# Five 128-row chunks instead of six 96-row chunks for k and v of the later batches, with kv of two batches moved by one iteration

## The chip, the cores and the metric

The kernel runs on one core of one Trainium2 chip. The metric is the device time in microseconds (us); lower is better. Each time quoted is a median of several executions. Engines are named as in the profile: PE is TensorE (PEld its weight loads), DVE is VectorE, ACT is ScalarE, POOL is GpSimd, SP is SyncE. "L144" is line 144 of the kernel file; the change adds lines, so the same line of code has another number after it.

## The reference

```python
# q, k, v: (8 batches, 8 heads, 576 tokens, 64), float32
kv  = np.einsum('bhsd,bhse->bhde', k, v)          # 64x64 per head, summed over 576 tokens
out = np.einsum('bhsd,bhde->bhse', q, kv)
rms = np.sqrt(np.mean(out * out, axis=-1, keepdims=True) + 1e-06)
x   = (out / rms * g_norm)                        # then put into (4608, 512)
y   = ((x @ w_a) * (x @ w_b)) @ w_out             # 512 -> 1536 -> 512
```

The change touches only the first line: the product of k and v of each head, and how k and v reach it.

## The kernel before: the parts that matter

The feed-forward part (FFN) works in nine strips of 512 tokens. The attention of batch s+1 is woven into strip s, so that its small matmuls and its work on the other engines hide under the FFN matmuls. Batches 0 and 1 are called early, the others late. k and v are loaded by POOL, which casts them from float32 to bf16 on the way, with the 576 tokens of a head as 96 partitions times 6 tokens:

```python
EC, EP = 6, 96
def load_heads(b, t, src, hs):
    nc.gpsimd.dma_start(out=t[:, hs, :, :],
        in_=src[b, hs].rearrange("h (t c) d -> t h c d", c=EC))

def load_late(b):                       # all of a late batch
    if b > EARLY:                       # wait until qT of the batch before has landed
        nc.gpsimd.tensor_copy(gate, qT[(b - 1) % 2][0:1, 0, 0:1])
    d = qs_d[b].rearrange("t (h d) -> t h d", h=H)
    for hs in (slice(0, NP), slice(NP, H)):
        nc.gpsimd.dma_start(out=d[:, hs, :], in_=q[b, hs].rearrange("h t d -> t h d"))
    load_heads(b, kt[b % NB], k, slice(0, H))      # NB = 3 buffers
    load_heads(b, vt[b % NB], v, slice(0, H))
# q goes to a bf16 copy in HBM (qs) and comes back by a DMA transpose into qT
```

kv of one pair of heads is a sum over the chunks. The two heads of a pair write different halves of the output's partitions:

```python
def kv(self, p, o):
    for c in range(EC):
        for j in range(2):
            nc.tensor.matmul(o[j * D : (j + 1) * D, :],
                lhsT=kt[self.b % NB][:, 2 * p + j, c, :],
                rhs=vt[self.b % NB][:, 2 * p + j, c, :],
                start=(c == 0), stop=(c == EC - 1))
```

With four pairs, a late batch needs 48 such matmuls, here called its kv block. The woven schedule of a strip has 16 iterations: the first 12 are FFN units of 8 matmuls each, the last 4 are output groups of 12:

```python
def slot(A, s, n):                      # called after the FFN work of iteration n
    k0, kn, xs = (4, 1, (6, 9, 11, 13)) if s < 3 else (2, 1, (4, 7, 10, 12))
    if n == k0: ...                     # the kv block, then its copy by ACT
    for p in range(NP):
        if n == xs[p]:                  # x(p): out of pair p into PSUM banks 4, 5; squares on ACT
            A.x(p, X[0]); A.psq(p, X[0])
        if n == xs[p] + 1:              # sum of squares on PE, 1/rms on ACT,
            A.pss(p, SS); A.pst(p, X[0])    # product on DVE, which frees banks 4, 5
```

Of the kernel before, what the change touches and what calls it, by code (L numbers as in the profile page):

```python
# [9 lines left out]
BF16 = mybir.dt.bfloat16  # L10
# [5 lines left out]
def kernel(  # L16
# [11 lines left out]
    nc = tc.nc  # L28

    B, H, S, D = q.shape  # L30
# [5 lines left out]
    NP = H // 2  # L36
# [5 lines left out]
    EC, EP = 6, 96  # L42
    EARLY = 2
# [5 lines left out]
    def sb(shape, dt, name):  # L49
        return pool.tile(shape, dt, name=name, tag=name)  # L50
# [5 lines left out]
    wb_v = moe_w_b.rearrange("(kc p) f -> p kc f", p=128)  # L56
    wo_v = moe_w_out.rearrange("(fc p) e -> p fc e", p=128)

    NB = 3
    kt = [sb([EP, H, EC, D], BF16, f"kt{i}") for i in range(NB)]  # L60
    vt = [sb([EP, H, EC, D], BF16, f"vt{i}") for i in range(NB)]
    qt = [sb([EP, H, EC, D], BF16, f"qt{i}") for i in range(EARLY)]

    qT = [sb([128, NP, S], BF16, f"qT{i}") for i in range(2)]
# [37 lines left out]
    def load_heads(b, t, src, hs):  # L102
        nc.gpsimd.dma_start(  # L103
            out=t[:, hs, :, :], in_=src[b, hs].rearrange("h (t c) d -> t h c d", c=EC)
        )

    def load_pair(b, p):
        hs = slice(2 * p, 2 * p + 2)
        load_heads(b, qt[b], q, hs)
        load_heads(b, kt[b % NB], k, hs)  # L110
        load_heads(b, vt[b % NB], v, hs)

    def load_ab(c0, c1):
        nc.gpsimd.dma_start(out=wa_t[:, :, c0:c1], in_=wa_v[:, :, c0:c1])
# [5 lines left out]
    def load_late(b):  # L120
        if b > EARLY:

            nc.gpsimd.tensor_copy(gate, qT[(b - 1) % 2][0:1, 0, 0:1])  # L123
        d = qs_d[b].rearrange("t (h d) -> t h d", h=H)
        for hs in (slice(0, NP), slice(NP, H)):
            nc.gpsimd.dma_start(out=d[:, hs, :], in_=q[b, hs].rearrange("h t d -> t h d"))  # L126
        load_heads(b, kt[b % NB], k, slice(0, H))
        load_heads(b, vt[b % NB], v, slice(0, H))

    def transpose_q(b):  # L130
        nc.sync.dma_start_transpose(qT[b % 2], qs_d[b])
# [2 lines left out]
    class Attn:  # L134
# [4 lines left out]

        def kv(self, p, o):  # L140

            for c in range(EC):
                for j in range(2):
                    nc.tensor.matmul(  # L144
                        o[j * D : (j + 1) * D, :],
                        lhsT=kt[self.b % NB][:, 2 * p + j, c, :],
                        rhs=vt[self.b % NB][:, 2 * p + j, c, :],
                        start=(c == 0),
                        stop=(c == EC - 1),
                    )  # L150

        def kv_out(self, ps, src):
# [77 lines left out]
    class Unit:  # L230
        n = 0
# [82 lines left out]
    def dummy(n, i, cols=STRIP):  # L314
        for _ in range(n):
            nc.tensor.matmul(
                P[:, i, 0:cols], lhsT=zeros[:, 0:128], rhs=zeros[:, 0:cols], start=True, stop=True
            )
# [15 lines left out]
    nc.vector.memset(ones, 0.0)  # L334
    for t in kvb:
        nc.vector.memset(t, 0.0)
    nc.vector.memset(ones[0:D, 0:D], 1.0 / D)
    nc.vector.memset(ones[D : 2 * D, D : 2 * D], 1.0 / D)
    for p in range(1, NP):
        load_pair(0, p)  # L340
# [8 lines left out]
    for p in range(NP):  # L349
        load_pair(1, p)  # L350
    load_late(2)

    X, SS = (4, 0), 6


    A = Attn(0)
# [9 lines left out]
    t = P[:, 2, :].bitcast(BF16)[:, 0:S].rearrange("q (c t) -> q c t", c=EC)  # L366
# [4 lines left out]
    for c in range(EC):  # L371
        nc.tensor.matmul(
            P[:, SS, 0 : 2 * D],
            lhsT=kc0[:, c, :],
            rhs=vc[:, c, :],
            start=(c == 0),
            stop=(c == EC - 1),
# [10 lines left out]
    for p in range(1, NP):  # L388
        i = X[p % 2]
        A.kv1(p, 3 - p % 2)  # L390
        A.kv1_out(p, 3 - p % 2, nc.vector.tensor_copy)
        A.pss(p - 1, SS)
        if p < NP - 1:
            if p == 1:
                dummy(1, 2 + p % 2)
            A.qtr(p + 1, 3 - p % 2)
            A.qtr_out(p + 1, 3 - p % 2)
            A.pst(p - 1, X[(p - 1) % 2])
            A.px(p, i)
            A.psq(p, i)  # L400
            dummy(1 if p == 1 else 2, 2 + p % 2)
# [30 lines left out]
    A = Attn(1)  # L432
# [30 lines left out]
    def slot(A, s, n):  # L463

        kb = P[:, 7, 0 : NP * D].rearrange("q (p e) -> q p e", e=D)
        k0, kn, xs = (4, 1, (6, 9, 11, 13)) if s < 3 else (2, 1, (4, 7, 10, 12))
        if k0 <= n < k0 + kn:
            for p in range((n - k0) * NP // kn, (n - k0 + 1) * NP // kn):
                A.kv(p, kb[:, p, :])
            if n == k0 + kn - 1:  # L470
                A.kv_out(slice(0, NP), kb)
        for p in range(NP):
            if n == xs[p]:
                A.x(p, X[0])
                A.psq(p, X[0])
            if n == xs[p] + 1:
                A.pss(p, SS)
                A.pst(p, X[0])

    for s in range(1, N_STRIP - 1):  # L480
        b = s + 1
        A = Attn(b) if b < B else None
        for n in range(FC + 4):
            if n >= FC:
                i = O if n % 2 == 0 else n_ab[0] % 3
                n_ab[0] += n % 2
                ffn_o(s, n - FC, i)
            elif s > 1 or n > 1:
                ffn_ab(s, n)
            if A:  # L490
                slot(A, s, n)
            if n == 8 and b + 1 < B:
                if s > 1:
                    transpose_q(b + 1)
                    if b + 2 < B:
                        load_late(b + 2)
                else:
                    load_late(3)
        if s == 1:
            transpose_q(3)  # L500
            load_late(4)
# [43 lines left out]
```

## Time and profile before

| | before |
|---|---|
| median of the first 3 executions | 323.02 us (322.78 to 323.4) |
| profiled span | 321.1 us |
| PE busy | 98% |
| kv block of a late batch, 48 matmuls | 0.88 us |
| wait of PE for v of batch 2 | 0.40 us |

The page of the kernel before. In the first part the columns are busy us, share of the span and number of instructions. The rows of the second part give the span in 40 slices of 8 us, in tenths busy (PEclk: tenths of the full clock that were granted).

```profile
span 321.1 us, 4773 instructions
...
PE 313.3 (98%) x1896; PEld 151.2 (47%) x1931; DVE 123.9 (39%) x215; ACT 125.3 (39%) x216; POOL 60.3 (19%) x82
...
PEclk9999999999999999999999999999999999999999
DMA  8999999796369999595597150003000200020002
```

PE is full from the second slice on, at full clock. The DMA engines are at 90% or more almost without a break until about 61 us. So a us counts if it is taken from PE's own stream, or from one of the few waits of PE that are left. The wait of PE that matters here, with its sum, count and longest in us:

```profile
PE P L144 <- DMA vt<-in_v_dram: 0.4, 1, 0.4
```

The chain of waits before, in order of time (start, length in us, and what held the chain), around batches 2 and 3. "PE P L144 x48" stands for 48 instructions of line 144 on PE that write P, the tile in PSUM. L144 is kv, L221 is x, L195 the sum of squares, L241 the FFN:

```profile
45.77 14.00 DMA vt<-in_v_dram
59.82 0.95 PE P L144 x48
...
64.33 0.24 PE P L221 x2
...
70.00 0.24 PE P L221 x2
...
73.94 0.36 PE P L221 x2
...
94.03 0.88 PE P L144 x48
...
104.14 0.24 PE P L221 x2
```

The DMA of v of batch 2 took from 45.77 us to its landing at 59.77 us, and the kv block of batch 2 (59.82 us) came after the wait for it. The block of batch 3 (94.03 us) followed on other PE work, and took 0.88 us. The first x of batch 2 took 0.24 us (64.33 us) and so did the second (70.00 us; for batch 3 it is the piece at 104.14 us); the third took 0.36 us (73.94 us).

The DMA view before, for 40 to 43 us (mostly packets of q, k and v of batch 1, 768 B written each), for 45 to 50 us (mostly packets of q of batch 2, 128 B), and for 58 to 60 us, where q1 (mostly the transpose of q) meets the end of v (on q0). Each line gives packets, MB, and the summed time of the packets as a share of 16 engines' time; it passes 100% where packets overlap on an engine:

```profile
q0 software_dynamic: 847, 0.60, 131.7%
```
```profile
q0 software_dynamic: 4598, 0.74, 201.4%
```
```profile
q1 hardware_dynamic: 1132, 0.29, 102.8%
q0 software_dynamic: 118, 0.08, 26.2%
```

### The profile page before, as it was taken

To read this page: it belongs to the slowest core of one execution; us is meant where nothing else is said; L and a number is where in the kernel's file an instruction comes from. 1 tells how busy PE (TensorE), PEld (TensorE's weight loads), DVE (VectorE), ACT (ScalarE), POOL (GpSimd) and SP (SyncE) were. 2 spreads that over 40 slices of the span, in tenths; PEclk is the share of its full clock that TensorE was granted. 3 is DMA by queue.
4 is the path that set the end of the run, shared out by engine and by line. 5 is a ranking of instruction groups with operands and counts; after the bars stand their busy time and mean duration, and the time that the engine had idled before them with its cause. 6 is when DMAs were issued, how large, how long until landed. Compare 5 with 4: busy or idle time off the path is not lost.

```text
span 321.1 us, 4773 instructions
## 1 busy us (share of the span) xinstructions
PE 313.3 (98%) x1896; PEld 151.2 (47%) x1931; DVE 123.9 (39%) x215; ACT 125.3 (39%) x216; POOL 60.3 (19%) x82
## 2 busy tenths in 40 slices
PE   8899999999999999999999999999999999999995
PEld 3444454444444444444444445444444444444443
DVE  3543344344234423452244424532354243313421
ACT  3633165354334433542355325433454233123310
POOL 8944870230041150410050000000000000000000
PEclk9999999999999999999999999999999999999999
DMA  8999999796369999595597150003000200020002
GB/s 179 196 196 199 201 179 230 140 136 117 96 92 162 119 162 216 63 160 113 140 109 115 65 133 8 0 35 99 2 0 0 100 33 0 25 90 20 0 35 98
DMA packets 69902, 32.61 MB, mean 102 GB/s; under 512 B 43639, under 2 KB 65399, under 8 KB 69879
## 3 DMA queue, kind: packets, MB, share of 16 engines
q0 software_dynamic: 49712, 18.44, 48.7%
q1 hardware_dynamic: 19810, 13.44, 16.3%
q10 hardware_dynamic: 356, 0.43, 0.4%
q8 instruction: 15, 0.25, 0.3%
q14 instruction: 9, 0.07, 0.1%
HBM read 37.75 MB, written 12.98 MB: 158 GB/s over the span
## 4 chain that ended last, share of the span: by engine, by line
PE 80%; DMA 13%; POOL 4%; issue 1%; ACT 0%; POOLq 0%
PE P L241 49%; PE P L291 26%; DMA wb_t<-in_moe_w_b_dram 6%; DMA vt<-in_v_dram 4%; PE P L221 2%; PE P L195 2%; DMA qt<-in_q_dram 2%; PE P L144 2%; DMA wo_t<-in_moe_w_out_dram 2%; POOL qs L126 1%; POOL kt L103 1%; POOL vt L103 1%; POOL wo_t L118 0%; POOL wa_t L344 0%; POOL wb_t L344 0%
## 5 line engine op out<-in xcount | busy, mean ns | idle before, releaser
L259 DVE TENSOR_TENSOR ab<-P,asb 128x512 bf16<-128x512 f32 x108 | 74.5, 692 | 124.9 <-PE P L241 123.9
L241 PE MATMUL P<-xt,wa_t 128*128 128x512 bf16 x422 | 111.2, 379 | 0.9 <-issue 0.2
L241 PE MATMUL P<-xt,wb_t 128*128 128x512 bf16 x419 | 110.0, 379 | 0.4
L291 PE MATMUL P<-wo_t,ab 128*128 128x512 bf16 (+1 forms) x433 | 97.3, 373 | 0.6
L255 ACT CAST asb<-P 128x512 bf16<-128x512 f32 x108 | 63.0, 585 | 81.9 <-PE P L241 80.5
L241 PEld LDWEIGHTS <-wb_t 128*128 128x128 bf16 x432 | 42.3, 98 | 51.2 <-DMA wb_t<-in_moe_w_b_dram 0.4
L291 PEld LDWEIGHTS <-ab 128*128 128x128 bf16 x444 | 43.1, 98 | 45.6
L241 PEld LDWEIGHTS <-wa_t 128*128 128x128 bf16 x432 | 41.7, 98 | 44.4 <-issue 0.5
L209 DVE SCALAR_TENSOR_TENSOR xt<-P,g_col,rs 128x288 bf16<-128x288 f32 x64 | 30.1, 513 | 24.2 <-ACT rs L199 24.2
L199 ACT ACTIVATE rs<-P,eps_t 128x576 f32<-128x576 f32 (+1 forms) x33 | 23.9, 726 | 21.2 <-PE P L195 17.2
L304 ACT COPY osb<-P 128x512 f32<-128x512 f32 x17 | 9.9, 585 | 48.6 <-PE P L291 46.8
L191 ACT ACTIVATE sq<-P 128x576 bf16<-128x576 f32 x31 | 20.2, 650 | 20.0 <-PE P L221 18.0
L306 DVE COPY osb<-P 128x512 f32<-128x512 f32 x18 | 12.4, 692 | 32.4 <-PE P L291 30.1
L126 POOL DMA_DIRECT2D qs<-in_q_dram x12 | 19.6, 1633 | 1.8 <-issue 1.7
L123 POOL COPY gate<-qT 1x1 bf16<-1x1 bf16 x5 | 0.9, 176 | 91.9 <-DMA qT<-qs 91.9
L195 PE MATMUL P<-sq,ones 128*128 128x288 bf16 x64 | 13.2, 286 | 0.5 <-ACT sq L191 0.4
L221 PE MATMUL P<-qT,kvb 128*128 128x288 bf16 x56 | 11.7, 286 | 0.0
L155 ACT CAST kvb<-P 64x256 bf16<-64x256 f32 (+1 forms) x20 | 6.0, 301 | 12.5 <-PE P L144 12.4
L195 PEld LDWEIGHTS <-ones 128*128 128x128 bf16 x64 | 6.2, 98 | 7.4 <-issue 0.4
L103 POOL DMA_DIRECT2D vt<-in_v_dram x13 | 9.1, 697 | 0.7 <-DMA qt<-in_q_dram 0.5
L103 POOL DMA_DIRECT2D kt<-in_k_dram x13 | 9.2, 705 | 0.1
L144 PEld LDWEIGHTS <-kt 96*64 96x64 bf16 x372 | 7.2, 112 | 3.9 <-issue 3.8
(46 smaller groups left out, 65.6 us busy)
## 6 DMA issues: line engine op xcount, KB each, us to landing
out_dram<-osb SPq DMA_DIRECT2D x23, 256.0 KB, 2.0
qs<-in_q_dram POOLq DMA_DIRECT2D x12, 288.0 KB, 6.7
kt<-in_k_dram POOLq DMA_DIRECT2D x6, 576.0 KB, 8.4
vt<-in_v_dram POOLq DMA_DIRECT2D x6, 576.0 KB, 10.8
out_dram<-osb SPq DMA_DIRECT2D x13, 128.0 KB, 2.3
wo_t<-in_moe_w_out_dram POOLq DMA_DIRECT2D x12, 128.0 KB, 6.0
wa_t<-in_moe_w_a_dram POOLq DMA_DIRECT2D x5, 256.0 KB, 9.3
wb_t<-in_moe_w_b_dram POOLq DMA_DIRECT2D x5, 256.0 KB, 9.9
```

The source lines that it names most:

```text
L103: nc.gpsimd.dma_start(out=t[:, hs, :, :], in_=src[b, hs].rearrange("h (t c) d -> t h c d", c=EC))
L126: nc.gpsimd.dma_start(out=d[:, hs, :], in_=q[b, hs].rearrange("h t d -> t h d"))
L144: nc.tensor.matmul(o[j * D : (j + 1) * D, :], lhsT=kt[self.b % NB][:, 2 * p + j, c, :], rhs=vt[self.b % NB][:, 2 * p + j, c, :], start=(c ...
L191: nc.scalar.activation(sq[p % 3], P[:, i0 : i0 + 2, 0:HF], AF.Square)
L195: nc.tensor.matmul(P[:, i0 + h, 0:HF], lhsT=ones, rhs=sq[p % 3][:, h, :], start=True, stop=True)
L199: nc.scalar.activation(rs[p % 3][:, h0:h1, :], P[:, i0 + h0 : i0 + h1, 0:HF], AF.Abs_reciprocal_sqrt, bias=eps_t,)
L209: nc.vector.scalar_tensor_tensor(out=xt[p][:, t0 : t0 + HF], in0=P[:, x0 + h, 0:HF], scalar=g_col, in1=rs[p % 3][:, h, :], op0=ALU.mult, o ...
L221: nc.tensor.matmul(P[:, i0 + h, 0:HF], lhsT=kvb[self.b % 2][:, p, :], rhs=self.qT[:, p, h * HF : (h + 1) * HF], start=True, stop=True,)
L241: nc.tensor.matmul(self.a if w is wa_t else self.b, lhsT=w[:, kc, self.fc * 128 : (self.fc + 1) * 128], rhs=xt[kc][:, t0 : t0 + STRIP], st ...
L255: nc.scalar.copy(self.t, self.a)
L259: nc.vector.tensor_mul(abt[self.s % 2][self.fc], self.b, self.t)
L291: nc.tensor.matmul(P[:, i, e0:e1], lhsT=abt[s % 2][fc][:, g * 128 : (g + 1) * 128], rhs=wo_t[:, fc, e0:e1], start=(fc == 0), stop=(fc == F ...
```

## The change

Its intent: a matmul is meant to cost by its columns, so the 576 tokens should go through in as few chunks as the 128 partitions allow. Four chunks of 128 tokens and a remainder of 64, padded by zeros to 128 rows, make 5 chunks instead of 6, so 40 matmuls per kv block instead of 48. As the loads get more packets, kv of batches 2 and 3 comes one iteration later, and with it their first x, x(0). One copy in the start moves from DVE to ACT.

```diff
-    NB = 3
-    kt = [sb([EP, H, EC, D], BF16, f"kt{i}") for i in range(NB)]     # vt alike
+    kt = [sb([EP, H, EC, D], BF16, f"kt{i}") for i in range(EARLY)]  # vt alike
+    LC = S // 128
+    ktl = [sb([128, H, LC + 1, D], BF16, f"ktl{i}") for i in range(2)]  # vtl alike
 ... in load_late
-        load_heads(b, kt[b % NB], k, slice(0, H))
-        load_heads(b, vt[b % NB], v, slice(0, H))
+        n = 128 * LC
+        for t, src in ((ktl[b % 2], k), (vtl[b % 2], v)):
+            nc.gpsimd.dma_start(out=t[:, :, 0:LC, :],
+                in_=src[b, :, 0:n].rearrange("h (t c) d -> t h c d", c=LC))
+            nc.gpsimd.dma_start(out=t[0 : S - n, :, LC, :],
+                in_=src[b, :, n:].rearrange("h t d -> t h d"))
 ... in kv
-            for c in range(EC):
+            if self.b < EARLY:
+                kk, vv, rows = kt[self.b], vt[self.b], [EP] * EC
+            else:
+                kk, vv, rows = ktl[self.b % 2], vtl[self.b % 2], [128] * (LC + 1)
+            for c, n in enumerate(rows):
 ... in the start
+    for t in ktl + vtl:
+        nc.vector.memset(t[S - 128 * LC :, :, LC, :], 0.0)
-        A.kv1_out(p, 3 - p % 2, nc.vector.tensor_copy)
+        A.kv1_out(p, 3 - p % 2, nc.scalar.copy if p == NP - 1 else nc.vector.tensor_copy)
 ... in slot
-        k0, kn, xs = (4, 1, (6, 9, 11, 13)) if s < 3 else (2, 1, (4, 7, 10, 12))
+        k0, kn, xs = (5, 1, (7, 9, 11, 13)) if s < 3 else (2, 1, (4, 7, 10, 12))
```

(Cuts are marked by lines that begin with "..."; lines are joined where that saves space.)

More of the change, by code (lines that the diff above doesn't have):

```diff
@@ L57 @@
     wo_v = moe_w_out.rearrange("(fc p) e -> p fc e", p=128)
-    NB = 3
-    kt = [sb([EP, H, EC, D], BF16, f"kt{i}") for i in range(NB)]
-    vt = [sb([EP, H, EC, D], BF16, f"vt{i}") for i in range(NB)]
+    kt = [sb([EP, H, EC, D], BF16, f"kt{i}") for i in range(EARLY)]
+    vt = [sb([EP, H, EC, D], BF16, f"vt{i}") for i in range(EARLY)]
+    LC = S // 128
+    ktl = [sb([128, H, LC + 1, D], BF16, f"ktl{i}") for i in range(2)]
+    vtl = [sb([128, H, LC + 1, D], BF16, f"vtl{i}") for i in range(2)]
     qt = [sb([EP, H, EC, D], BF16, f"qt{i}") for i in range(EARLY)]
@@ L109, in load_pair @@
         load_heads(b, qt[b], q, hs)
-        load_heads(b, kt[b % NB], k, hs)
-        load_heads(b, vt[b % NB], v, hs)
+        load_heads(b, kt[b], k, hs)
+        load_heads(b, vt[b], v, hs)
     def load_ab(c0, c1):
@@ L126, in load_late @@
             nc.gpsimd.dma_start(out=d[:, hs, :], in_=q[b, hs].rearrange("h t d -> t h d"))
-        load_heads(b, kt[b % NB], k, slice(0, H))
-        load_heads(b, vt[b % NB], v, slice(0, H))
+        n = 128 * LC
+        for t, src in ((ktl[b % 2], k), (vtl[b % 2], v)):
+            nc.gpsimd.dma_start(
+                out=t[:, :, 0:LC, :],
+                in_=src[b, :, 0:n].rearrange("h (t c) d -> t h c d", c=LC),
+            )
+            nc.gpsimd.dma_start(
+                out=t[0 : S - n, :, LC, :], in_=src[b, :, n:].rearrange("h t d -> t h d")
+            )
     def transpose_q(b):
@@ L145, in kv @@
                         o[j * D : (j + 1) * D, :],
-                        lhsT=kt[self.b % NB][:, 2 * p + j, c, :],
-                        rhs=vt[self.b % NB][:, 2 * p + j, c, :],
+                        lhsT=kk[0:n, 2 * p + j, c, :],
+                        rhs=vv[0:n, 2 * p + j, c, :],
                         start=(c == 0),
-                        stop=(c == EC - 1),
+                        stop=(c == len(rows) - 1),
                     )
```

## The prediction

> **What bounds the kernel.** TensorE. The page gives PE 98% busy at a granted clock of 0.998; DVE and ACT 39%. PE's waits are small: 0.4 us for the DMA of v, 0.4 for wb at 16.45 us, some more in the start. The DMA engines are full only until about 61 us. So only time in PE's stream counts, or the wait for v.
>
> **Removed.** In the chain of waits a kv block of a late batch (48 matmuls of 96x64) takes 0.88 us (0.95 in batch 2), 18.3 ns per matmul; the displayed 196 ns overlap. 40 at the same spacing is 0.73 us. The Trainium skill, "TensorE: Matmul & The Clock Gate", section "LDWEIGHTS (loading the stationary operand)", says that a weight load costs by its columns, not its rows; so 128 rows should cost what 96 do (no run here shows it yet). Saving 0.15 us x 6 = 0.9 us, all on the critical path.
>
> **Moved: kv of batch 2.** Before, PE waits 0.40 us at 59.42 for v of batch 2, which lands at 59.8. Now kv comes 8 FFN matmuls (1.73 us) later, at about 61.1. x(0) moves along. If v has landed by then, the 0.40 us goes.
>
> **Added: DMA packets.** k and v of a batch were 768 packets each, of 768 B written (1,536 read). Now they are 1,024 of 512 B plus 512 of 128 B. In the DMA view of 40 to 43 us the 768 B packets go at about 260 per us (0.20 MB written per us); at 45 to 50 us the 128 B packets of q go at about 870 per us. Estimate: 2.9 us per tensor becomes 2.6 + 0.6, so 0.6 us more for the two if alone. But output stores run from 51 us and the transpose of q moves packets from 58 us, so the last 128 B packets alternate with it. I estimate 0.6 to 2 us: v lands at 60.4 to 61.8, against a need at 61.1. Hence a wait of 0 to 0.7 us, 0.3 expected, in place of the 0.40. The Trainium skill, "DMA: Bandwidth & Descriptors", section "Specifications", gives 512 B as the least for line rate: the main part is just there, the remainder below. POOL issues about 3 us instead of 1.55 us per late batch; it has slack. Later batches are loaded some 30 us ahead: no effect.
>
> **Nothing from the rest.** Four memsets on DVE (about 0.3 to 0.6 us each) fit in its 3 us wait for q at the start. The last kv copy of batch 0: 204 ns for 64 columns on ACT against 210 on DVE, and DVE is free 0.05 us after the matmuls anyway. Even a gain would end in PE's wait for wb at 16.45 us: DMA bounds the start.
>
> **Sum.** 323.0 - 0.9 - 0.40 + 0.3 = 322.0 us. Range 321.2 to 322.9. Chances: faster by over 2% 0.01, within 2% 0.98, slower by over 2% 0.01.
>
> **What would show it.** Right: kv blocks of 40 matmuls in about 0.73 us; PE's wait before kv of batch 2 between 0 and 0.7 us; v's DMAs longer to landing; chain until 16.5 us as before. Wrong: blocks still 0.88 us (the spacing grows with rows); over 1 us of wait at kv of batch 2, or at its fifth chunk, which waits for the remainder's own DMA; PE waiting for k or v of a later batch.
>
> **What would make it wrong.** Small packets sharing the engines worse than estimated, so that v of batch 2 lands at 63 us or later; the transpose of q (landed 61.8 before) delayed beyond x(0) at about 65.5; memsets running past 5.07 us and delaying the first cast of q.

## The result

| | before | after |
|---|---|---|
| median, 6 executions each | 323.26 us | 322.41 us |
| range | 322.78 to 323.6 | 322.1 to 323.67 |
| profiled span | 321.1 us | 320.7 us |

The ratio of after to before is 0.9984, with a 95% interval of 0.9962 to 1.0005. Ratios here are the mean time of one kernel's fast runs over that of the other's of the same rounds, so they are not quite the ratios of the medians. So the gain is about 0.5 us by the ratio, 0.85 us by the medians and 0.4 us by the two profiles, and by time alone it can't be told from nothing. The profile can tell more, as the parts repeat to some hundredths of a us. The page after:

```profile
span 320.7 us, 4732 instructions
...
DMA  8999999999359999899799150003000200020002
```

The DMA engines are now at 90% or more in eight of the first nine slices, before in seven. The busy sums of PE are not compared, as some records of matmuls were missing from the trace of before (422 and 419 of 432 FFN matmuls were there). The wait of PE for v is still there:

```profile
PE P L158 <- DMA vtl<-in_v_dram: 0.5, 1, 0.5
```

The chain of waits after (L158 is kv, L235 x, L209 the sum of squares, L255 the FFN):

```profile
47.29 14.47 DMA vtl<-in_v_dram
...
61.80 0.69 PE P L158 x32
...
66.06 0.24 PE P L235 x2
...
70.00 0.36 PE P L235 x2
...
95.88 0.75 PE P L158 x40
...
104.14 0.36 PE P L235 x2
```

Three things are to be read here. A kv block of 40 matmuls takes 0.75 us instead of 0.88 us. The block of batch 2 is cut: the chain enters it with 32 of its 40 matmuls, released by the DMA of v. And the second x of a strip, the piece at 70.00 us and the one at 104.14 us, now takes 0.36 us where before it took 0.24 us.

The matmuls of PE in order of time, after (start, length, in brackets the idle time before):

```profile
61.03 0.32 PE L158 MATMUL P<-vtl,ktl 128*64 128x64 bf16 x8
61.80 0.69 PE L158 MATMUL P<-vtl,ktl 128*64 128x64 bf16 x32 [0.46 <-DMA vtl<-in_v_dram]
...
69.84 0.53 PE L235 MATMUL P<-qT,kvb 128*128 128x288 bf16 x2
```

PE ran the first 8 matmuls of the block, the four main chunks of the first pair. Then it stood 0.46 us for the fifth chunk, whose 64 rows come by a DMA of their own. The DMA view after, for 58 to 60 us:

```profile
q1 hardware_dynamic: 776, 0.20, 88.6%
q0 software_dynamic: 498, 0.11, 57.1%
```

Against the same window before, the queue of k and v (q0) is not nearly done: it still moved 498 packets here instead of 118. The other queue, mostly the transpose, moved 776 packets instead of 1,132.

### The profile page after: what moved, and what is told of

It is laid out like the page before. It is cut to its first block, busy times and chain, and to the rows that moved or that the text cites. A ratio compares the mean times of both kernels' runs of the same rounds, so it can differ in the third digit from the quotient of the medians.

```text
span 320.7 us, 4732 instructions
## 1 busy us (share of the span) xinstructions
PE 315.0 (98%) x1883; PEld 150.6 (47%) x1883; DVE 124.9 (39%) x218; ACT 125.5 (39%) x217; POOL 70.0 (22%) x94
## 4 chain that ended last, share of the span: by engine, by line
PE 80%; DMA 12%; POOL 6%; issue 1%; ACT 0%; POOLq 0%
PE P L255 49%; PE P L305 26%; DMA wb_t<-in_moe_w_b_dram 6%; DMA vtl<-in_v_dram 5%; PE P L235 2%; PE P L209 2%; DMA qt<-in_q_dram 2%; PE P L158 1%; POOL qs L129 1%; POOL vt L106 1%; POOL wo_t L121 1%; POOL qt L106 1%; POOL kt L106 1%; POOL wb_t L360 0%; POOL wa_t L360 0%
## 5 line engine op out<-in xcount | busy, mean ns | idle before, releaser
L255 PE MATMUL P<-xt,wa_t 128*128 128x512 bf16 x432 | 111.9, 379 | 0.0
L255 PE MATMUL P<-xt,wb_t 128*128 128x512 bf16 x432 | 111.7, 379 | 0.0
L255 PEld LDWEIGHTS <-wb_t 128*128 128x128 bf16 x432 | 42.3, 98 | 51.0 <-DMA wb_t<-in_moe_w_b_dram 0.2
L255 PEld LDWEIGHTS <-wa_t 128*128 128x128 bf16 x432 | 41.7, 98 | 44.7 <-issue 0.5
L205 ACT ACTIVATE sq<-P 128x576 bf16<-128x576 f32 x31 | 20.1, 650 | 20.4 <-PE P L235 18.3
L209 PE MATMUL P<-sq,ones 128*128 128x288 bf16 x64 | 13.2, 286 | 0.5 <-ACT sq L205 0.4
L235 PE MATMUL P<-qT,kvb 128*128 128x288 bf16 x56 | 11.9, 286 | 0.0
L209 PEld LDWEIGHTS <-ones 128*128 128x128 bf16 x64 | 6.2, 98 | 7.4 <-issue 0.4
L235 PEld LDWEIGHTS <-kvb 128*128 128x128 bf16 x56 | 5.5, 98 | 6.0
L330 PE MATMUL P<-zeros 128*128 128x512 bf16 x17 | 6.9, 547 | 1.2 <-DVE eps_t L345 1.2
L121 POOL DMA_DIRECT2D wo_t<-in_moe_w_out_dram x12 | 6.4, 531 | 6.7 <-DMA wb_t<-in_moe_w_b_dram 3.3
```

What stands on the lines that cost most here:

```text
L205: nc.scalar.activation(sq[p % 3], P[:, i0 : i0 + 2, 0:HF], AF.Square)
L209: nc.tensor.matmul(P[:, i0 + h, 0:HF], lhsT=ones, rhs=sq[p % 3][:, h, :], start=True, stop=True)
L235: nc.tensor.matmul(P[:, i0 + h, 0:HF], lhsT=kvb[self.b % 2][:, p, :], rhs=self.qT[:, p, h * HF : (h + 1) * HF], start=True, stop=True,)
L255: nc.tensor.matmul(self.a if w is wa_t else self.b, lhsT=w[:, kc, self.fc * 128 : (self.fc + 1) * 128], rhs=xt[kc][:, t0 : t0 + STRIP], st ...
```

## The experiments

All were correct against the reference except one, which is marked. Runs of the kernel before: medians of 323.24 us for e1 to e4, 322.9 us for e6 to e9, 323.43 us for e5, e11 and e12. Where the intervals of two ratios overlap, the times alone do not rank the two kernels.

### e1: x of strips 1 and 2 where it was

```diff
-        k0, kn, xs = (5, 1, (7, 9, 11, 13)) if s < 3 else (2, 1, (4, 7, 10, 12))
+        k0, kn, xs = (5, 1, (6, 9, 11, 13)) if s < 3 else (2, 1, (4, 7, 10, 12))
```

> The changed kernel with the first x of strips 1 and 2 at iteration 6 again instead of 7, so that x(0) and x(1) are three iterations apart as in the kernel before; kv stays at iteration 5. Theory A (the second x waits for the DVE products of the first when they are two iterations apart): the matmuls of x(1) take 0.24 us instead of 0.36 in the chain, in both strips, and the profiled span is about 0.22 us under the 320.7 of the changed kernel, so about 320.5; timed about 0.07% better than the change. Rival B (the 0.36 us have another cause, such as the banks of PSUM or the position in the iteration): x(1) stays at 0.36 us. Risk: x(0) now comes about 1.7 us after kv, and the transposed q lands at about 63.1 us against a need at 64.2 us; if it is late a new wait shows there.

Measured: median 321.97 us against 323.24 us, ratio 0.9957 (0.9924 to 0.999), span 320.3 us. The same pieces of its chain:

```profile
69.81 0.24 PE P L235 x2
...
73.76 0.36 PE P L235 x2
...
103.83 0.25 PE P L235 x2
```

The second x takes 0.24 and 0.25 us again in the two strips (69.81 and 103.83 us), the third still 0.36 us. The transposed q was in time. Theory A holds. The span fell by 0.4 us where 0.22 us was expected; 0.16 us of that PE was ahead already at 57 us, before any edited line runs. The cause can be seen on DVE after the change, in order of time:

```profile
69.08 0.94 DVE L223 SCALAR_TENSOR_TENSOR xt<-P,g_col,rs 128x288 bf16<-128x288 f32 x2 [0.26 <-ACT rs L213]
```

The products that free the PSUM banks of x(0) end at 69.08 + 0.94 = 70.02 us, while x(1) begins at 69.84 us. Its second matmul writes the bank that is still being read: in the trace that DVE instruction releases it at 70.04 us, and it starts at 70.08 us, 0.24 us after the first, where the two start 0.12 us apart in e1. With two iterations between x(0) and x(1), the way from the sum of squares (67.86 us) over ACT and DVE is a little longer than one FFN unit; with three iterations it hides. The third x had this loss before as well.

### e2: the new loads, without the later iteration

```diff
-        k0, kn, xs = (5, 1, (7, 9, 11, 13)) if s < 3 else (2, 1, (4, 7, 10, 12))
+        k0, kn, xs = (4, 1, (6, 9, 11, 13)) if s < 3 else (2, 1, (4, 7, 10, 12))
```

> The changed kernel with kv and x of strips 1 and 2 at their old iterations (4; 6, 9, 11, 13): the new loads without the later slot. Theory A (the added packets delay v of batch 2 by about 2 us, and the later slot only pays for that): PE reaches kv at 59.3 us and waits until about 61.7 us, so a wait of 2.0 to 2.3 us in place of 0.46; span about 1.5 us over the changed kernel, about 322.2. Rival B (v lands when it did before, about 59.8 us, and the 0.46 us of the changed kernel have another cause): wait of 0.4 to 0.5 us, span about 320.5.

Measured: median 324.15 us, ratio 1.0035 (0.9992 to 1.0078); the profiled execution was the slowest of the six (327.51 us, span 325.6 us). PE's matmuls in it:

```profile
61.04 0.32 PE L158 MATMUL P<-vtl,ktl 128*64 128x64 bf16 x8 [1.58 <-DMA vtl<-in_v_dram]
62.33 1.07 PE L158 MATMUL P<-vtl,ktl 128*64 128x64 bf16 x32 [0.97 <-DMA vtl<-in_v_dram]
63.33 1.89 PE L255 MATMUL P<-xt,wa_t 128*128 128x512 bf16 x4
```

PE waited 1.58 us for the main part of v and 0.97 us more for the remainder, 2.55 us in all, a little over the 2.0 to 2.3 us expected: v lands at about 62.3 us here, against 59.8 us before. That is 2.5 us later, and rival B falls. In the six profiles with the new loads in this order v landed between 61.27 us (e4) and 63.37 us (e5); in the two with the old loads at 59.77 us (before) and 60.21 us (e3). The span was missed by 3.4 us for a second reason, which is seen in the same view: the FFN matmuls from 63.33 us on take twice their time. The table by stretches (busy us of PE, PEld, DVE, ACT, POOL with counts, then the granted clock, the DMA share and GB/s) shows why:

```profile
60.00:62.00 2.00, 0.32 (x8) 0.20 (x8) 0.26 (x1) 0.00 (x0) 0.00 (x0) 0.91 1.36 106
62.00:64.00 2.00, 1.67 (x34) 1.21 (x34) 0.00 (x0) 0.56 (x2) 0.18 (x1) 0.50 0.49 99
...
66.00:68.00 2.00, 2.00 (x7) 0.62 (x6) 0.69 (x1) 0.00 (x0) 2.00 (x3) 0.50 0.98 63
68.00:70.00 2.00, 2.00 (x11) 0.97 (x10) 0.42 (x1) 0.83 (x2) 2.00 (x3) 0.89 1.89 121
```

The granted clock fell to 0.50 and came back after 68 us. The 0.91 of the first stretch puts the fall at about 61.6 us (0.09 of 2 us is 0.36 us at half clock), an estimate from this table: after the pause of 1.58 us, 8 small matmuls and the first 0.3 us of the second pause. That is one execution; of the five others, four were granted 1.0 and one 0.998, and they took 323.4 to 324.3 us, 0.2 to 1.1 us over the median of before. So a wait of PE in this place can cost more than its own length, as it did in one execution of six.

### e3: the later iteration, without the new loads

```diff
 # in the kernel before
-        k0, kn, xs = (4, 1, (6, 9, 11, 13)) if s < 3 else (2, 1, (4, 7, 10, 12))
+        k0, kn, xs = (5, 1, (7, 9, 11, 13)) if s < 3 else (2, 1, (4, 7, 10, 12))
```

> The kernel before with only the iterations of the change (kv at 5, x at 7, 9, 11, 13), loads and chunks untouched. Theory A: v lands at about 59.8 us as before, kv starts at about 61.1 us without any wait (gain 0.40 us), and x(1) takes 0.36 us instead of 0.24 in two strips (loss 0.22 us): span about 320.9 against 321.1, kv blocks 0.88 us. Rival B (v lands late because of where kv stands, not because of packets): a wait of about 0.4 us at kv again, and span 321.3.

Measured: median 322.65 us, ratio 0.9976 (0.994 to 1.0012), span 320.8 us. The five executions lie within 322.51 to 322.76 us, the closest of all kernels here; this fits a kernel whose PE no longer meets the uneven landing of v, but as proof five executions are few. PE at kv of batch 2:

```profile
61.04 0.95 PE L144 MATMUL P<-vt,kt 96*64 96x64 bf16 x48
```

There is no wait before kv, and the second x takes 0.36 us in both strips. Theory A holds. The moved iteration alone, with six chunks, reaches a span of 320.8 us against the 320.7 us of the whole change (ratios 0.9976 and 0.9984; both intervals reach past 1, so the times alone show no difference of either from the kernel before).

### e4: six chunks of 128 rows

```diff
-                kk, vv, rows = ktl[self.b % 2], vtl[self.b % 2], [128] * (LC + 1)
+                kk, vv, rows = ktl[self.b % 2], vtl[self.b % 2], [128] * (LC + 2)
 ... in the loop over chunks and j
+                    if c > LC and self.b >= EARLY:
+                        nc.tensor.matmul(o[j * D : (j + 1) * D, :], lhsT=zeros[:, 0:D],
+                            rhs=zeros[:, 0:D], start=False, stop=True)
+                        continue
```

> The changed kernel with a sixth chunk in each late kv that multiplies 128 rows of zeros (the result stays right): 48 matmuls per block with 128 rows. Theory A (a kv block costs by the number of matmuls, 16 to 18 ns each, rows are free): blocks of 0.87 to 0.89 us as in the kernel before, that is 0.13 us more than the 0.75 of the change, times six, so span 0.7 to 0.8 us over the change, about 321.4. Rival B (rows cost, and part of the saving went into wider loads): blocks over 0.92 us.

Measured: median 323.21 us, ratio 0.9993 (0.9962 to 1.0024), span 321.0 us. One block in its chain (L167 the chunks, L159 the zeros), with the FFN (L264) that follows:

```profile
124.60 0.28 PE P L167 x10
124.88 0.03 PE P L159 x2
...
125.48 3.56 PE P L264 x16
```

From 124.60 to 125.48 us the 48 matmuls take 0.88 us, as the 48 of 96 rows did before. So 128 rows cost no more than 96 here, and 8 matmuls are worth 0.13 us, 16 ns each. The span grew by 0.3 us and not by 0.7, because v of batch 2 landed earlier in this execution: FFN went on at 62.07 us, against 62.43 us in the profile of the change, and five blocks at 0.13 us less 0.36 us are those 0.3 us.

### e5: the last kv copy of batch 0 on DVE

```diff
-        A.kv1_out(p, 3 - p % 2, nc.scalar.copy if p == NP - 1 else nc.vector.tensor_copy)
+        A.kv1_out(p, 3 - p % 2, nc.vector.tensor_copy)
```

> The changed kernel with the last kv copy of batch 0 on VectorE again. Theory A (the copy takes 0.21 us on either engine and the start is bound by DMA anyway): PE's first FFN matmul moves by 0.05 us at most, and from 17 us on nothing differs; span within 0.3 us of the change. Rival B (the copy on ACT is part of the gain): span 0.3 us or more above the change.

Measured: median 322.46 us, ratio 0.9983 (0.9955 to 1.0012), the same as the change. From the start of the kv matmuls to the start of the x that needs the copy it took 0.70 us (13.40 to 14.10 us), against 0.69 us in the change (13.34 to 14.03). The profiled span was 322.3 us, 1.6 us over the change and outside what was expected. That profile had longer waits for DMAs:

```profile
PE P L158 <- DMA vtl<-in_v_dram: 1.2, 2, 0.9
PE P L255 <- DMA wb_t<-in_moe_w_b_dram: 0.5, 1, 0.5
```

PE was already 0.75 us behind the change at ACT's first cast of an FFN result (18.46 against 17.71 us), and v landed at 63.37 us. That the copy on DVE does not cause this is seen in the kernel before and in e3, which have it too and reached the same point at 17.53 and 17.65 us. The other executions of e5 went down to 321.95 us. So the copy is worth nothing that these runs could see. The execution does show how far the waits for wb and v swing from one run to the next, for a cause that stays open.

### e6: the remainder DMAs first

```diff
-        for t, src in (k, v): main DMA; remainder DMA
+        for t, src in (k, v): remainder DMA
+        for t, src in (k, v): main DMA
```

> The changed kernel, with the two remainder DMAs of each late batch (512 packets of 128 B each) issued ahead of the two main ones: the same packets, in another order. Theory A (v lands late because its last 128 B packets alternate with the packets of the transpose, one for one): the tail is now 512 B packets, the small ones run before the transpose starts; v lands about 0.5 to 1 us earlier, and the wait at kv of batch 2 falls from 0.46 us to 0 to 0.2; span about 320.3. Rival B (only the sum of the added work counts, not its order): v's last DMA lands at about 61.7 us as in the change, and as the first matmul now needs it the wait is 0.5 to 0.8 us; span 320.7 to 321.0.

Measured: median 322.29 us (4 executions), ratio 0.9977 (0.9959 to 0.9995), span 320.1 us. PE at kv of batch 2:

```profile
61.09 0.82 PE L160 MATMUL P<-vtl,ktl 128*64 128x64 bf16 x40
```

There is no wait in this profile: v landed at 60.79 us, against 61.76 us in the change, which is theory A's side. But one profile does not settle it: in e11, with the same order, v landed at 61.37 us, and in e4, with the order of the change, at 61.27 us.

What the tail costs can be read in the trace of the change. The remainder of v landed after the main part by 1.31 us in batch 2 (60.45 to 61.76 us), by 1.31 and 2.14 us in batches 4 and 5, and by 0.43 to 0.45 us in batches 3, 6 and 7. The DMA view of that stretch for batch 2, then for batch 3 (78.16 to 78.61 us), where q1 moved nothing:

```profile
q1 hardware_dynamic: 698, 0.18, 126.9%
q0 software_dynamic: 36, 0.00, 5.1%
```
```profile
q0 software_dynamic: 26, 0.00, 10.7%
```

In batches 4 and 5 q1 moved 719 and 723 packets meanwhile, in 6 and 7 at most 18. In the five other profiles with this order (e1, e2, e4, e5, e12) the tail took 0.74 to 1.32 us in batches 2, 4 and 5 and 0.16 to 0.77 us in the others, but for one of 1.75 us. So the tail is longer where it meets the transpose. The two queues do not alternate one for one, as the expectation had it: 36 packets of q0 stand against 698 of q1. The Trainium skill, "DMA: Bandwidth & Descriptors", section "Queues, rings and completion order", says that a DMA engine goes round-robin between the queues that have work, a whole packet of several descriptors at a time. Whether the profile's packets are those packets or their descriptors no run here shows, so the result fits this rule and does not test it.

### e7 and e8: k and v of batch 2 before its q

```diff
 # load_late, for batch 2 only: the two DMAs of q are issued after those of k and v
 # e8: also xs = (6, 9, 11, 13) as in e1
```

> The changed kernel, with k and v of batch 2 issued before q of batch 2 (nothing else moved). Theory A (the wait at kv of batch 2 is the end of a full DMA queue, and q of batch 2 is needed later than k and v): no wait at kv of batch 2, so the 0.46 us go; the transposed q lands later, at 64 to 65.5 us, against a need at 65.9; span about 320.2, and the spread between runs shrinks, as the run with only the later slot had (0.25 us). Rival B: q is now the late one, and PE waits for it at x(0) instead: a new wait of up to 1 us there.

> The run before this one with x(0) of strips 1 and 2 at iteration 6 again. Theory A: x(0) needs the transposed q at about 63.7 us, and it lands at 64 to 65.5 us: the 0.22 us won at x(1) are lost again in a wait of 0.3 to 1.5 us at x(0) of batch 2; span 320.2 to 321. Rival B (q lands before 63.7): span about 319.9.

Measured: e7 median 322.79 us, ratio 0.9992 (0.9973 to 1.0011), span 321.0 us; e8 median 323.99 us, ratio 1.0043 (1.0014 to 1.0072), span 321.8 us. The waits of PE in e7, then in e8 (L241 is the line of x in these two kernels):

```profile
PE P L241 <- DMA qT<-qs: 0.7, 1, 0.7
```
```profile
PE P L241 <- DMA qT<-qs: 1.9, 1, 1.9
```

The wait for v is gone in both, and a wait for q has come in its place, longer where x(0) comes earlier. In e7 both what theory A expected at kv and what rival B expected at x(0) came true. In e8 the wait of 1.93 us was longer than the 0.3 to 1.5 us expected, and two of its six executions had granted clocks of 0.993 and 0.995 (326.57 and 325.55 us). The queue holds so much work until 61 us; moving whole tensors ahead only chose who waits. Nor did the spread of e7 shrink as expected (322.38 to 324.02 us).

### e9: batch 2 in the old layout (wrong result)

```diff
+        if b == EARLY:      # batch 2 into the buffers of batch 0
+            load_heads(b, kt[0], k, slice(0, H)); load_heads(b, vt[0], v, slice(0, H))
+            return
 ... kv reads these buffers in six chunks for batch 2; xs = (6, 9, 11, 13) as in e1
```

> The changed kernel with batch 2 alone loaded as in the kernel before (six chunks of 96 rows, in the buffers that batch 0 has left), batches 3 to 7 in five chunks, and x of strips 1 and 2 at iterations 6, 9, 11, 13. Theory A (the new layout costs only where the DMA queue is full, that is for batch 2): v of batch 2 lands at about 59.8 us, no wait at kv at 61.0 us, x(1) at 0.24 us, five blocks at 0.75 and one at 0.88 us: span about 0.6 us under the change, about 320.1, timed 321.6 to 321.8, with a small spread. Rival B: span 320.5 or more.

Measured: wrong (relative error 0.48), 370.85 us. The likely fault is the edit's: the loads of batch 2 are written ahead of the arithmetic of batch 0 in the program, so that batch 0 waits for them and reads them. The wait in the trace fits this:

```profile
PE P L162 <- DMA vt<-in_v_dram: 46.5, 1, 46.5
```

PE waited 46.5 us in the start for them. It tells nothing of either theory.

### e11 and e12: both remedies, and the change again

```diff
 # e11: the change, with the order of e6 and xs = (6, 9, 11, 13) of e1
 # e12: the change, unaltered
```

> The changed kernel with both remedies found so far: the remainder DMAs issued ahead of the main ones, and x of strips 1 and 2 at iterations 6, 9, 11, 13. Theory A (the two losses are independent): no wait at kv of batch 2, x(1) at 0.24 us in both strips, the transposed q (landed at 62.3 us when only the order of the DMAs was changed) in time for x(0) at 63.6 us: span about 319.9, timed 321.4 to 321.8, 0.2 to 0.3% under the change run in the same rounds, and about 0.45% under the kernel before. Rival B: a new wait for q at x(0), span 320.3 or more.

> The changed kernel again, unaltered, on the same chip as the others of this call: how far its profile and its time repeat. Theory A (the remaining spread comes from when v of batch 2 lands): kv blocks at 0.75 us and x(1) at 0.36 us to the hundredth, as in the first profile, while the wait at kv of batch 2 differs by some tenths from the first 0.46 us; ratio to before 0.997 to 0.999.

Measured: e11 median 321.94 us, ratio 0.9954 (0.9933 to 0.9974), span 320.2 us. e12 median 322.73 us, ratio 0.9997 (0.9959 to 1.0036), span 320.6 us; one of its executions took 326.54 us, which pulls up the mean. The wait at kv of batch 2 in e11, then in e12:

```profile
PE P L160 <- DMA vtl<-in_v_dram: 0.3, 1, 0.3
```
```profile
PE P L158 <- DMA vtl<-in_v_dram: 0.2, 1, 0.2
```

In e11, x(1) took 0.24 us and the blocks 0.75 us, but v was late by 0.31 us in this execution, where in e6 it was not. So the span missed the expected 319.9 us, and the median the expected 321.8 us, narrowly. In e12 the blocks and the x repeated to the hundredth and the wait was 0.24 us instead of 0.46 us, as expected of it. e11 is the fastest version together with e1 (0.9957). Against e12 it is 0.2% ahead by the medians; by the ratios it is more, for the one slow execution, which also put e12 above the 0.997 to 0.999 expected. That the order of the remainders adds anything in time to what e1 gives is not shown, nor that it brings v forward in every execution.

## Why the prediction was right or wrong

The median measured lies in the range (321.2 to 322.9 us), 0.4 us above the point of 322.0 us. That says little for the account: the upper end of the range is only 0.4 us under the median of the kernel before (323.26 us), and by the profiles the gain is under half of the 1.0 us predicted. One step was wrong and two were mis-sized, and they happened to add up to a loss that the range still holds. The span fell by 0.4 us. In us of the profiles, this is how it comes about:

| step | predicted | measured |
|---|---|---|
| kv blocks of batches 3 to 7 | -0.73 (5 x 0.147) | -0.65 (5 x 0.13) |
| batch 2: block, and wait for v | -0.25 (-0.15 - 0.40 + 0.30) | +0.05 |
| x(1) in strips 1 and 2 | 0 | +0.22 (2 x 0.11) |
| the start until 54 us | 0 | -0.05 |
| sum | about -1.0 | about -0.4 |

For batch 2, FFN work went on at 60.70 us before and at 62.43 us after, 1.73 us later; that is exactly the FFN unit that now stands in front of it, and PE had come 0.05 us earlier.

- **"128 rows should cost what 96 do": right.** e4 shows it: 0.88 us for 48 matmuls with either. The Trainium skill, "TensorE: Matmul & The Clock Gate", section "LDWEIGHTS (loading the stationary operand)", has it so for the weight load, and the runs agree: its median is 113 ns with 96 rows and with 128.
- **"Saving 0.15 us x 6": a little too large.** The mean of 18.3 ns per matmul includes about 0.1 us per block that does not scale. The slope between 40 and 48 matmuls is 16 ns (0.13 us over 8). The sixth block, that of batch 2, saved nothing to be seen, since it stands behind the wait.
- **"0.3 expected, in place of the 0.40": right in kind, too small.** The wait was 0.46 us, at the fifth chunk, as the prediction named it. v landed at 61.76 us, 2.0 us later than before, at the far end of "0.6 to 2 us". In e2, where nothing hid this, PE waited 2.55 us. The Trainium skill, "DMA: Bandwidth & Descriptors", section "Specifications", gives 512 B as the least for line rate; the runs show the cost of the 128 B remainder as the tail after the main part (1.31 us beside the transpose, 0.43 to 0.45 us without it, see e6), not as a rate. The main part itself landed at 60.45 us, in time.
- **"v's DMAs longer to landing": true of the load as a whole, not of the line on the page.** In batch 2 it holds: 14.00 us before, 14.47 us after for the remainder, which was issued 1.5 us later. But the page's median over all late batches went from 10.8 to 10.0 us: the page lists only the main DMAs in that line, which have fewer bytes. From the issue of k to the landing of the last of v, the load took longer in all six batches: by 2.1, 1.55 and 2.3 us in batches 2, 4 and 5, whose tails met the transpose, and by 0.05 to 0.4 us in the others, where 0.6 us was estimated for a load alone. Nor are the DMA engines "full only until about 61 us": the row of the page shows them full again in slices 13 to 16.
- **"x(0) moves along": this is the step that failed.** It is true that x(0) keeps its distance from kv. But x(0) then stands two iterations before x(1) instead of three, and that costs 0.11 us in each of the two strips. The chain of before already showed it: the third x, two iterations after the second, took 0.36 us. e1 undoes this one number and gets the 0.22 us back.
- **"Nothing from the rest": right.** The memsets took 0.55 us per pair on DVE, which then still waited 1.7 us for q. The copy on ACT made no difference (e5). PE arrived at 54 us within 0.05 us of before.
- **"Later batches: no effect": right.** No wait for k or v of batches 3 to 7 shows.

So the gain of the fifth chunk was real, 0.13 us per batch, and for the batch whose loads end in the full DMA queue it was paid back by the loads. By the profiles, the moved iteration alone gives 0.3 us (e3) and the whole change 0.4 us; on top of the moved iteration, the chunks win 0.65 us of PE in five blocks and return 0.5 us of it at batch 2, as a new wait. The spacing of x took 0.22 us from either. With x put back (e1), the change is faster than the kernel before by 0.4%, and its interval lies below 1.

What stays open: why v lands some tenths of a us earlier or later in executions of the same kernel, and why single executions of several kernels took 2 to 4 us more at a clock of 1.0.

## What to carry to other kernels

When a piece of work is moved in a woven schedule, price both of its distances: to what it needs, and to what comes next and needs its buffer. Fewer matmuls by another data layout must be charged with the packets of that layout at the moment when the DMA queue is fullest, and a tail of small packets that PE waits for should be kept away from other traffic (1.31 us beside the transpose, 0.45 us without); issuing it first is worth trying (e6), though its gain is not shown here. A wait on a busy PE can cost more than its own length if the clock falls (in one execution of e2), so a schedule with slack at the one late load may be worth as much as a faster instruction stream.

## What the Trainium skill lacked or had wrong

- "TensorE: Matmul & The Clock Gate", the table of the two clock states in Part 1 and "Why this matters for your kernels": the half clock is said to follow an idle window of about 3.4 us, or gaps over about 3 us. In e2 the granted clock fell to 0.50 about 0.3 us into the second of two pauses (1.58 us and 0.97 us, with 8 small matmuls between them), that is some 2.2 us after the last FFN matmul before them, and it stayed there for over 6 us; e8, whose profiled wait was 1.93 us at full clock, had granted clocks of 0.993 and 0.995 in two other executions.
- The same page, "Wait — 56ns, not 53.3ns?": start to start is said never to drop below about 25 ns, with no exception named there for matmuls on different columns of the array (Part 3 of the page has such matmuls start about 4 ns apart). Here, with 64-column matmuls on alternate halves of the output's partitions, each with a weight load of its own, the starts in a kv block alternate between 3 to 4 ns (to the other half) and 28 to 29 ns (back to the first), 16 ns on the mean; so the sentence holds here within a half, and not from one half to the other.
- No page (it would belong to "DMA: Bandwidth & Descriptors") gives rates for casting DMAs of small packets. Here packets of 128 B written and 256 B read (q, from HBM to HBM) went at about 870 per us (4,347 packets under 512 B in 5 us, among 251 larger ones), and ones of 768 B written and 1,536 B read (into SBUF) at about 260 per us (783 in 3 us, among 64 small ones), with no other queue moving data but for one instruction packet.
